# Five tiles from seven products to eight, and row loads moved in the order of issue, in a Fourier layer followed by a squared-ReLU MLP

## The chip, the cores and the metric

The kernel runs on one core of a Trainium2 chip. The metric is the time on the device for one execution, in microseconds (us), lower is better. Engines: TensorE (PE in the profile; PEld is its weight load), VectorE (DVE), ScalarE (ACT), GpSimd (POOL) and SyncE (SP), which here only issues DMAs.

## The reference

```python
def _attn_ref(x, w_r, w_i, b_r, b_i):          # x: 8 x 3008 x 256
    X = np.fft.rfft(x, axis=1)
    Yr = X.real @ w_r - X.imag @ w_i + b_r
    Yi = X.real @ w_i + X.imag @ w_r + b_i
    lam = 0.01
    Yr = np.sign(Yr) * np.maximum(np.abs(Yr) - lam, 0.0)
    Yi = np.sign(Yi) * np.maximum(np.abs(Yi) - lam, 0.0)
    return np.fft.irfft(Yr + 1j * Yi, n=x.shape[1], axis=1)

def _moe_ref(x, w_in, w_out, s, b):            # x: 24064 x 256, w_in: 256 x 2048, w_out: 2048 x 256
    r = np.maximum(x @ w_in, 0.0)
    return (s * (r * r) + b) @ w_out
```

A Fourier transform along the sequence of each of eight batches, a complex matrix product with a soft threshold per frequency, the transform back, and then for all 24064 tokens a two-layer network whose activation is a squared ReLU.

## The kernel before

**The Fourier part.** 3008 = 94 x 32, so a transform is done in steps of small matrix products, batch by batch. Step 1 (`s1_units`, 16 units a batch) multiplies x by a 94-point table and stores the rows `u` to a scratch `ud` in DRAM. `take_rows` (L640) loads them back in another order, as four tiles `us` (384 KB each), from a pool of four buffers. Steps 2 and 3 (`s23_units`) do the 32-point transform, reading `us[(b, i // 3)]` for the i-th of 12 forward units, the complex product, the threshold (`shrink`, in a ring of tiles, with small SBUF to SBUF DMAs) and the inverse 32-point transform, and store `v` to `vd` in DRAM. After the last inverse unit two loads bring `vd` back as the two halves `vs` (768 KB each, a pool of two). Step 4 (`s4_units`, 14 groups) does the inverse 94-point transform from them into `yt`: groups 0 to 5 read the first half alone, group 6 reads both.

**The network part.** The tokens are cut into 48 tiles of 384 to 512 tokens (`_tile_order`); batches 0 and 1 have six tiles each, later ones five, and the leftovers of two batches make two tail tiles. `first_mm` does a tile's product with `w_in`, 16 blocks of 128 hidden units, into two banks of PSUM (`psh`); ScalarE takes the ReLU to `rt` (L867), and ScalarE (L877) or VectorE (L880) squares it into `gt`. The product with `w_out` follows one tile later, and in one of two ways:

- `second_mms`, eight products: 64 matmuls of 256 columns, `gt` against `w_out_t`, and two additions of the bias (L941) to the output tile `ost`, two stores each, after slots 7 and 15.
- `seven_mms`, the Strassen-Winograd form: 112 matmuls of 128 columns with sums of blocks on both sides. The weight sums (`T_s`) are made once. The sums of `gt` are made for each tile in `s_op`: three additions on VectorE (L976) and one accumulating DMA issued by POOL (`gt<-gt`, L969, 256 KB) for each half of the tile, two of the additions at slots 10 and 11 of the tile's first product, the rest in slots 2 to 5 of the next. `leave` recombines the seven products on VectorE in eight additions (L1008) and one more (L1026), in slots 4, 6, 11 and 15; the four stores follow in slot 15.

`seven(ti)` says which tiles take the second way, 22 of 48: 4 to 7, 10, 11, 15, 16, 18, 21, 22, 24, 27, 30, 33, 34, 36, 39, 41 to 43 and 45.

**The order.** Everything is one instruction stream an engine, written out by hand in slots: 16 slots a tile, one block of `first_mm` each. In a slot come first what `plan` holds for it, then `first_mm` of this tile, then a share of the second product of the tile before. `mark[b]` is the slot at which batch b's first tile begins: 0, 96, 192, 272, 368, 464, 560, 656. For batch b (2 to 7), with s0, s1, s2 = mark[b-2], mark[b-1], mark[b]: step 1 runs from s0 + 36 to s1 - 14, `take_rows` stands at s1 - 9, steps 2 and 3 run from s1 + 2 to s2 - 28, step 4 in the last 15 slots before s2. The tiles s1/16 - 2 and s1/16 - 1 go by seven wherever they have 480 or 512 tokens.

**Who evacuates.** `evac` and the squares pick ScalarE or VectorE while the stream is written: a planner keeps a running load for each of the two (`load`), raised to `pe["now"]`, TensorE's own running time, and takes the one that would be done first, with a lead of 0.4 us for ScalarE.

All loads and stores named here but x and the accumulates are issued by SP, in stream order; an SP issue waits for its own data and buffers only.

Of the kernel before, what the change touches and what calls it, by code (L numbers as in the profile page):

```python
# [9 lines left out]
F16 = mybir.dt.float16  # L10
# [6 lines left out]
N2 = 32  # L17
# [79 lines left out]
def kernel(  # L97
# [521 lines left out]
    def s1_units(b, more_banks=False):  # L619

        ud = dpool.tile([96, N2, D], F16, name="ud", tag="ud")
        hold = {}

        def unit(i):
            c, j = divmod(2 * i, XCH)
            k = j % UCH
            if k == 0:
                hold["u"] = upool.tile([P, UCH, D], F16, name="u", tag="u")
            ps = any_bank() if more_banks else one_bank()
            matmul(  # L630
                ps[0:96, :], A_t[0:N1, :], x16[(b, c)][0:N1, j * D : (j + 2) * D],
                start=True, stop=True,
            )
            u = hold["u"]
            evac(u[0:96, k : k + 2, :], ps[0:96, :].rearrange("p (j d) -> p j d", j=2), 512)
            if k == UCH - 2:
                n = 2 * i + 2
                nc.sync.dma_start(out=ud[:, n - UCH : n, :], in_=u[0:96])

        def take_rows():  # L640
            uv = ud.rearrange("k n d -> (k n) d").rearrange("(q p) d -> p q d", p=P)
            for q in range(4):
                t = uspool.tile([P, 6, D], F16, name="us", tag="us")
                nc.sync.dma_start(out=t, in_=uv[:, 6 * q : 6 * q + 6, :])
                us[(b, q)] = t

        return [lambda i=i: unit(i) for i in range(N2 // 2)], take_rows

    def s23_units(b):

        vd = dpool.tile([NPAIR, P, D], F16, name="vd", tag="vd")
        if not ring:
            ring.append(bigpool.tile([P, 12, 2, D], F16, name="ring", tag="corr"))
        xf = {}
        zt = {}
        hold = {}

        def fwd_unit(i):

            bank = one_bank()  # L660
            ps = bank.rearrange("p (r c j k) -> p r c j k", r=2, c=DC, j=2)
            t = us[(b, i // 3)]
            for j in range(2):
                q = (2 * i + j) % 6
                for dc in range(DC):
                    matmul(
                        ps[:, :, dc, j, :], t[:, q, dc * P : (dc + 1) * P],
                        F_t[:, 2 * i + j, :], start=True, stop=True,
                    )
            xt = xfpool.tile([P, 3, DC, P], F16, name="xf", tag="xf")  # L670
            evac(xt[:, 1:3].rearrange("p r c k -> p (r c k)"), bank, 512)
            nc.vector.tensor_tensor(out=xt[:, 0], in0=xt[:, 1], in1=xt[:, 2], op=ALU.add)  # L672
            work("dve", 0.34)
            xf[i] = xt

        def sum_unit(h):

            ps = one_bank().rearrange("p (i e) -> p i e", i=2)
            for i in range(2):
                for dc in range(DC):  # L680
                    matmul(
                        ps[:, i, :], xf[2 * h + i][:, 0, dc], W_t[:, dc, 0],
                        start=(dc == 0), stop=(dc == DC - 1),
                    )
            s = mpool.tile([P, 2, D], F32, name="s", tag="m")
            nc.scalar.copy(out=s, in_=ps)
            work("act", 0.49)
            hold[h] = s

        def mix_unit(i):  # L690
            ps = one_bank().rearrange("p (r e) -> p r e", r=2)
            xt = xf.pop(i)
            for r in range(2):
                for dc in range(DC):
                    matmul(
                        ps[:, r, :], xt[:, 2 - r, dc], W_g[:, dc, r],
                        start=(dc == 0), stop=(dc == DC - 1),
                    )
            nc.vector.tensor_tensor(  # L699
                out=ring[0][:, i % 4], in0=ps,  # L700
                in1=hold[i // 2][:, i % 2].unsqueeze(1).to_broadcast([P, 2, D]), op=ALU.add,
            )
            work("dve", 0.67)
            if b == 1:
                shrink(i, 1)
            elif i % 2:
                shrink(i - 1, 2)

        def shrink(i, n):

            m0 = 4 + (i % 2 if n == 1 else 0)
            t, m = ring[0][:, i % 4 : i % 4 + n], ring[0][:, m0 : m0 + n]
            lo, hi = (v.unsqueeze(1).to_broadcast([P, n, 2, D]) for v in (low, high))
            nc.vector.tensor_tensor(out=m, in0=t, in1=lo, op=ALU.max)
            nc.vector.tensor_tensor(out=m, in0=m, in1=hi, op=ALU.min)
            nc.vector.tensor_tensor(out=t, in0=t, in1=m, op=ALU.subtract)
            work("dve", 0.21 + 0.8 * n)
            for k in range(i, i + n):
                z = ring[0][:, 6 + k % 6]
                for j in range(2):  # L720
                    for r in range(2):
                        o = z[64 * r : 64 * r + 64, j]
                        a = t[64 * j : 64 * j + 64, k - i, r]
                        if k < H - 2:
                            nc.sync.dma_start(out=o, in_=a)
                        else:
                            nc.vector.tensor_copy(out=o, in_=a)
                            work("dve", 0.13)
                zt[k] = z

        def inv_unit(i):
            ps = one_bank().rearrange("p (j e) -> p j e", j=2)
            z = zt.pop(i)
            for j in range(2):
                matmul(
                    ps[:, j, :], T_t[:, 2 * i + j, :], z[:, j, :], start=True, stop=True
                )
            if i % 2 == 0:
                hold["v"] = vpool.tile([P, 4, D], F16, name="v", tag="v")
            v = hold["v"]  # L740
            h = 2 * (i % 2)
            evac(v[:, h : h + 2, :], ps, 512)
            if i % 2 == 1:
                nc.sync.dma_start(
                    out=vd[2 * i - 2 : 2 * i + 2].rearrange("q p e -> p q e"), in_=v
                )
            if i == H - 1:
                vv = vd.rearrange("q (k n) e -> (q k) (n e)", n=N2)
                for h in range(2):
                    t = vspool.tile([96, HW, D], F16, name="vs", tag="vs")  # L750
                    nc.sync.dma_start(
                        out=t.rearrange("k n e -> k (n e)"),
                        in_=vv[:, h * HW * D : (h + 1) * HW * D],
                    )
                    vs[(b, h)] = t

        units = []

        def put(f, i, n):
            if 0 <= i < n:  # L760
                units.append(lambda: f(i))

        for h in range(H // 2 + 3):
            for i in range(2):
                put(fwd_unit, 2 * h + i, H)
                put(mix_unit, 2 * h - 2 + i, H)
                put(inv_unit, 2 * h - 6 + i, H)
            put(sum_unit, h, H // 2)
            if h == H // 2:
                units += [lambda: None] * 2  # L770
        return units

    def s4_units(b):

# [288 lines left out]
    def seven(ti):  # L1063
        if ti >= len(tiles) - 2 or not halves(ti):
            return False
        firsts = [mark[b] // MC for b in range(2, B)]
        return (
            ti >= firsts[-1] or 4 <= ti < 8 or any(m - 2 <= ti < m for m in firsts)
            or any(ti == m + 1 for m in firsts[1:])
        )  # L1070

    plan = {}
# [27 lines left out]
    plan.setdefault(52, []).append(lambda: emit_load_x(2, chunks=range(3, 4)))  # L1100
    for i in range(4):
        plan.setdefault(38 + 2 * i, []).append(lambda i=i: make_t(i))
    schedule(24, 42, s23_units(1))
    schedule(mark[1] - 12, 16, s4_units(1))
    for b in range(2, B):
        s0, s1, s2 = mark[b - 2], mark[b - 1], mark[b]
        p = s1 - s0
        units, take_rows = s1_units(b)
        schedule(s0 + 36, p - 50, units)
        plan.setdefault(s1 - 9, []).append(take_rows)  # L1110
        p = s2 - s1
        schedule(s1 + 2, p - 30, s23_units(b))
        schedule(s2 - 15 + (p < 90), 14 - (p < 90), s4_units(b))
        if b + 1 < B:
            for c, at in enumerate((10, 14, 26, 54)):
                plan.setdefault(s1 + at, []).append(
                    lambda b=b, c=c: emit_load_x(b + 1, chunks=range(c, c + 1))
                )
# [46 lines left out]
```

## Time and profile before

| | us |
|---|---|
| median of 3 runs | 844.29 |
| the three runs | 842.41, 844.29, 849.45 |
| the profiled execution | 843.5 |
| its span, first to last instruction | 841.7 |

| issued on | DMA | count | KB each |
|---|---|---|---|
| SP | us<-ud | 28 | 384 |
| SP | vs<-vd | 14 | 768 |
| POOL | gt<-gt | 40 and 4 | 256 and 240 |
| SP | ring<-ring | 280 | 32 |

Instructions stand as engine, operation, out<-in by tile names, shape and count; buffer numbers are left out. `psh`, `psa` and `psf` are pools of PSUM banks. All matmuls are recorded under one helper's line, L175, and evacuations under L187 (ScalarE) and L189 (VectorE), so they are told apart by tiles. An arrow `<-DVE ring L699` behind a line names what ended the idle time before it.

### The profile page before, as it was taken

What the parts mean: (1) busy time and instruction counts of PE and PEld (TensorE: products, weight loads), DVE (VectorE), ACT (ScalarE), POOL (GpSimd) and SP (SyncE); (2) the same over time, 40 slices, a digit from 0 to 9 for tenths busy, and PEclk for the clock granted to TensorE, in tenths of its full rate; (3) what the DMA queues carried; (4) which work ended last, traced back from release to release, by engine and by line L of the source; (5) the groups of instructions that cost most, each with busy time, mean ns of one, the idle gap of its engine ahead of it and who ended that gap; (6) DMA issues with size and microseconds to landing.
All of it is one profiled execution on the core that took longest, in us unless ns stands there. A gap on an engine that the chain in (4) does not pass through costs nothing.

```text
span 841.7 us, 19681 instructions
## 1 busy us (share of the span) xinstructions
PE 823.0 (98%) x7710; PEld 599.3 (71%) x7710; DVE 718.2 (85%) x1120; ACT 722.1 (86%) x959; POOL 87.7 (10%) x116
## 2 busy tenths in 40 slices
PE   8999999999999999999999999999999999999997
PEld 7857767777677767776677666777667767767765
DVE  5988989998898888888888888788889888879885
ACT  5998988998899988988899888889879898788882
POOL 4550001110010001100010000100001000001000
PEclk9999999999999999999999999999999999999999
DMA  8954587356873478436773458614565253513322
GB/s 199 180 152 102 124 195 193 63 104 151 202 177 66 107 173 215 105 90 143 188 184 70 96 137 206 168 53 108 131 175 142 51 109 99 144 45 76 71 64 62
DMA packets 116959, 107.70 MB, mean 128 GB/s; under 512 B 12806, under 2 KB 100874, under 8 KB 115522
## 3 DMA queue, kind: packets, MB, share of 16 engines
q1 hardware_dynamic: 102498, 80.55, 33.7%
q0 software_dynamic: 14368, 25.89, 19.4%
q8 instruction: 60, 0.98, 0.5%
q14 instruction: 33, 0.27, 0.1%
HBM read 53.52 MB, written 46.66 MB: 119 GB/s over the span
## 4 chain that ended last, share of the span: by engine, by line
PE 70%; DVE 11%; ACT 8%; DMA 6%; issue 3%; SPq 1%; POOL 0%; DVEq 0%; ACTq 0%; POOLq 0%
PE psh L175 29%; PE psa L175 25%; PE psf L175 15%; ACT rt L867 3%; DVE gt L880 2%; DVE gt L976 2%; ACT gt L877 2%; DMA vd<-v 1%; DMA ring<-ring 1%; DMA x<-in_x_dram 1%; DVE ring L699 1%; DMA vs<-vd 1%; PE psm L175 1%; DMA gt<-gt 1%; DVE s L976 1%
## 5 line engine op out<-in xcount | busy, mean ns | idle before, releaser
L867 ACT ACTIVATE rt<-psh 128x1024 f32<-128x1024 f32 (+2 forms) x384 | 387.0, 1009 | 66.5 <-PE psh L175 64.3
L175 PEld LDWEIGHTS <-gt 128*128 128x128 f16 (+1 forms) x3728 | 305.1, 101 | 167.7 <-DMA gt<-gt 1.2
L175 PE MATMUL psh<-yt,w_in 128*128 128x512 f16 (+1 forms) x1344 | 396.6, 378 | 0.1
L880 DVE TENSOR_TENSOR gt<-rt 128x1024 f16<-128x1024 f32 (+2 forms) x238 | 285.2, 1203 | 61.1 <-ACT rt L867 59.7
L175 PE MATMUL psa<-w_out_t,gt 128*128 128x256 f16 (+3 forms) x2432 | 305.9, 252 | 1.0 <-DMA gt<-gt 1.0
L877 ACT ACTIVATE gt<-rt 128x1024 f16<-128x1024 f32 (+2 forms) x146 | 151.7, 1039 | 3.5
L175 PEld LDWEIGHTS <-w_in 128*128 128x128 f16 x1536 | 136.2, 98 | 25.3 <-issue 2.6
L175 PE MATMUL psa<-T_s,gt 128*128 128x128 f16 (+1 forms) x992 | 83.4, 219 | 0.0
L969 POOL DMA_DIRECT2D gt<-gt x44 | 39.7, 902 | 379.7 <-DVE s L976 200.3
L699 DVE TENSOR_TENSOR ring<-psf,s 128x512 f16<-128x512 f32 x84 | 57.5, 685 | 3.5 <-PE psf L175 2.7
L187 ACT CAST u<-psf 96x512 f16<-96x512 f32 x91 | 52.6, 580 | 9.1 <-PE psf L175 8.9
L187 ACT CAST v<-psf 128x512 f16<-128x512 f32 x82 | 47.5, 582 | 11.1 <-PE psf L175 11.1
L175 PEld LDWEIGHTS <-xf 128*128 128x128 f16 x504 | 46.5, 98 | 8.7 <-DVE xf L672 1.9
L175 PE MATMUL psh<-tail,w_in 128*128 128x512 f16 (+1 forms) x192 | 52.1, 353 | 0.0
L175 PE MATMUL psf<-W_g,xf 128*128 128x256 f16 x336 | 50.4, 272 | 1.0 <-ACT xf L187 1.0
L234 POOL DMA_DIRECT2D x<-in_x_dram x36 | 19.2, 538 | 265.2 <-PE psf L175 264.1
L187 ACT CAST yt<-psf 128x470 f16<-128x470 f32 (+2 forms) x84 | 43.3, 534 | 4.1 <-PE psf L175 2.9
L1008 DVE SCALAR_TENSOR_TENSOR ost<-psa,s_bc,zz 128x256 f32<-128x256 f32 (+1 forms) x84 | 38.1, 479 | 7.2 <-PE psa L175 6.5
L941 DVE SCALAR_TENSOR_TENSOR ost<-psa,s_bc,bias_bc 128x512 f32<-128x512 f32 (+2 forms) x49 | 35.6, 726 | 6.9 <-PE psa L175 5.0
L175 PE MATMUL psf<-x,A_t 94*96 94x512 f16 x102 | 38.9, 381 | 2.0 <-ACT v L187 0.8
L175 PE MATMUL psf<-C_t,vs 96*128 96x94 f16 (+1 forms) x484 | 37.9, 205 | 0.8 <-DMA vs<-vd 0.8
L187 ACT CAST xf<-psf 128x512 f16<-128x512 f32 x62 | 36.2, 584 | 2.1 <-PE psf L175 1.9
(118 smaller groups left out, 810.7 us busy)
## 6 DMA issues: line engine op xcount, KB each, us to landing
out_dram<-ost SPq DMA_DIRECT2D x152, 128.0 KB
ud<-u SPq DMA_DIRECT2D x56, 192.0 KB
us<-ud SPq DMA_DIRECT2D x28, 384.0 KB
vd<-v SPq DMA_DIRECT2D x42, 256.0 KB
vs<-vd SPq DMA_DIRECT2D x14, 768.0 KB
x<-in_x_dram POOLq DMA_DIRECT2D x28, 376.0 KB, 6.1
gt<-gt POOLq DMA_DIRECT2D x40, 256.0 KB, 4.4
ring<-ring SPq DMA_DIRECT2D x280, 32.0 KB
```

The lines of the kernel that those rows point to most:

```text
L175: return nc.tensor.matmul(out, lhs, rhs, **how)
L187: return None, nc.scalar.copy(out=dst, in_=src)
L234: nc.gpsimd.dma_start(out=t[0:N1, i * w : (i + 1) * w], in_=xv[:, c * XCH * D + i * w : c * XCH * D + (i + 1) * w],)
L699: nc.vector.tensor_tensor(out=ring[0][:, i % 4], in0=ps, in1=hold[i // 2][:, i % 2].unsqueeze(1).to_broadcast([P, 2, D]), op=ALU.add,)
L867: nc.scalar.activation(out=rt[:, :, 0:w], in_=ps[:, :, 0:w], func=AF.Relu)
L877: nc.scalar.activation(out=gt, in_=rr, func=AF.Square)
L880: last_square[0] = nc.vector.tensor_tensor(out=gt, in0=rr, in1=rr, op=ALU.mult)
L941: nc.vector.scalar_tensor_tensor(out=ost[0:size, 0:k], in0=ps[0:size, 0:k], scalar=s_bc[0:size], in1=bias_bc[0:size].unsqueeze(1).to_broad ...
L969: nc.gpsimd.dma_start(out=a12, in_=a11, accum_op=ALU.add)
L976: nc.vector.tensor_tensor(out=out, in0=a, in1=b, op=op)
L1008: nc.vector.scalar_tensor_tensor(out=out, in0=of, scalar=s_bc[0:size], in1=other, op0=ALU.mult, op1=ALU.add)
```

## The change

```diff
-        def take_rows():
+        def take_rows(which=range(4)):
             uv = ud.rearrange("k n d -> (k n) d").rearrange("(q p) d -> p q d", p=P)
-            for q in range(4):
+            for q in which:
                 t = uspool.tile([P, 6, D], F16, name="us", tag="us")
                 nc.sync.dma_start(out=t, in_=uv[:, 6 * q : 6 * q + 6, :])
                 us[(b, q)] = t
...
             if i == H - 1:
-                vv = vd.rearrange("q (k n) e -> (q k) (n e)", n=N2)
-                for h in range(2):
-                    t = vspool.tile([96, HW, D], F16, name="vs", tag="vs")
-                    nc.sync.dma_start(
-                        out=t.rearrange("k n e -> k (n e)"),
-                        in_=vv[:, h * HW * D : (h + 1) * HW * D],
-                    )
-                    vs[(b, h)] = t
+                hold["vv"] = vd.rearrange("q (k n) e -> (q k) (n e)", n=N2)
+                take_half(0)
+                if b == 1:
+                    take_half(1)
+
+        def take_half(h):
+            t = vspool.tile([96, HW, D], F16, name="vs", tag="vs")
+            nc.sync.dma_start(
+                out=t.rearrange("k n e -> k (n e)"),
+                in_=hold["vv"][:, h * HW * D : (h + 1) * HW * D],
+            )
+            vs[(b, h)] = t
...
-        return units
+        return units, lambda: take_half(1)
...
         return (
-            ti >= firsts[-1] or 4 <= ti < 8 or any(m - 2 <= ti < m for m in firsts)
-            or any(ti == m + 1 for m in firsts[1:])
+            ti >= firsts[-1] or 4 <= ti < 7 or any(m - 2 <= ti < m for m in firsts)
         )
...
-        plan.setdefault(s1 - 9, []).append(take_rows)
+        for q, at in enumerate((-9, -6, -1, 4)):
+            plan.setdefault(s1 + at, []).append(lambda t=take_rows, q=q: t([q]))
         p = s2 - s1
-        schedule(s1 + 2, p - 30, s23_units(b))
+        units, take_half = s23_units(b)
+        schedule(s1 + 2, p - 30, units)
+        plan.setdefault(s2 - 23, []).append(take_half)
```

- Tiles 7, 18, 24, 30 and 36 go by eight products; 17 stay by seven. `m + 1` in the removed line is the second tile of batches 3 to 6 (tile 42 of batch 7 stays through `firsts[-1]`).
- For batches 2 to 7 the four row loads stand at slots s1 - 9, s1 - 6, s1 - 1 and s1 + 4.
- For batches 2 to 7 the second half of `vs` is loaded at slot s2 - 23, some five slots after the first; batch 1 keeps both together.

The planner's loads follow from the changed stream, so it may give other evacuations and squares to the two engines anywhere after tile 7.

More of the change, by code (lines that the diff above doesn't have):

```diff
@@ L1102 @@
         plan.setdefault(38 + 2 * i, []).append(lambda i=i: make_t(i))
-    schedule(24, 42, s23_units(1))
+    schedule(24, 42, s23_units(1)[0])
     schedule(mark[1] - 12, 16, s4_units(1))
```

## Prediction

> **What bounds the kernel now.** The page's first part comes first, for the share of each engine.
>
> ```profile
> PE 823.0 (98%) x7710; PEld 599.3 (71%) x7710; DVE 718.2 (85%) x1120; ACT 722.1 (86%) x959; POOL 87.7 (10%) x116
> ```
>
> TensorE is at 98%, so nearly every microsecond of matmul issue is a microsecond of the run. VectorE and ScalarE have room on average, so what they cost is seen only where TensorE pauses. I cut the run at the first matmul of each tile (48 stages; stage k holds the first product of tile k and the second product of tile k-1) and read the busy times by window. A stage named here by k starts at the start of its row.
>
> ```profile
> core 0: us, PE busy (x) PEld busy (x) DVE busy (x) ACT busy (x) POOL busy (x), PEclk, DMA share, GB/s
> ...
> 371.24:390.55 19.31, 18.41 (x191) 13.30 (x189) 16.77 (x28) 18.20 (x25) 2.26 (x3) 1.00 0.57 114
> 390.55:408.25 17.70, 17.70 (x127) 12.19 (x125) 16.28 (x27) 15.10 (x22) 0.54 (x1) 1.00 0.60 156
> ...
> 179.57:198.46 18.89, 18.12 (x191) 13.31 (x188) 16.48 (x31) 17.93 (x25) 2.26 (x3) 1.00 0.65 134
> 660.22:677.62 17.40, 17.40 (x139) 12.63 (x137) 14.70 (x24) 14.70 (x19) 0.00 (x0) 1.00 0.22 57
> 677.62:695.47 17.85, 16.85 (x187) 12.53 (x184) 14.88 (x25) 16.52 (x21) 1.71 (x2) 1.00 0.56 123
> ```
>
> Length, then TensorE busy. Stage 19 (371.24) runs the second product of tile 18 by seven: 0.90 idle. Stage 20 (390.55), with a second product by eight and the same kind of work beside it: none. Stages 8 and 37 follow tiles 7 and 36, which the change also takes: 0.77 and 1.00 idle. The clock is 1.00 throughout, so nothing is to be had there. The timeline of TensorE, where stage 19 pauses and where stage 20 runs by eight:
>
> ```profile
> 378.72 0.50 PE L175 MATMUL psa<-T_s,gt 128*128 128x128 f16 x6
> 379.67 0.38 PE L175 MATMUL psf<-ring,T_t 128*128 128x256 f16 x2 [0.46 <-DVE ring L699]
> ...
> 403.46 0.60 PE L175 MATMUL psa<-w_out_t,gt 128*128 128x256 f16 x4
> ```
>
> A record is longer than its issue interval, as matmuls overlap. Six of 128 columns last 0.50, the last of them 0.219 (mean of the form), so the interval is (0.50 - 0.219)/5 = 0.056. Four of 256 columns: (0.60 - 0.272)/3 = 0.109. After six at 0.056 the next could start at 379.06; it started at 379.67, so 0.61 of issue was lost, though only 0.46 shows as idle. Summed this way from the starts, the lost issue is 1.54 in stage 8, 1.55 in each of 19, 25 and 31 and 1.16 in 37: 7.35 us. Why that one pause came is in the chain of waits in order of time:
>
> ```profile
> 374.56 0.60 DVE gt L976
> 375.16 0.61 DVE s L976
> 375.80 0.70 DVE gt L976
> 376.60 0.62 DVE gt L976
> ...
> 379.02 0.61 DVE ring L699
> ...
> 533.38 7.93 DMA gt<-gt
> ```
>
> The four L976 are the sums by seven products of tile 18. They stand in VectorE's order ahead of the ring addition that the matmul waits for. The last line is another matter: an accumulating DMA of tile 27, for which TensorE waited 1.2 us at 541.36.
>
> **The change part by part.** All against the profiled 843.5 us.
>
> Five tiles back to eight (7, 18, 24, 30, 36). Matmul issue: 112 x 0.056 = 6.27 leave, 64 x 0.109 = 6.98 come, +0.71 a tile, **+3.55** on the path, since TensorE has no room. VectorE, a tile: six sums at 0.687 (4.12), seven additions at 0.479 (3.35), one at 0.748 and one at 0.416 leave; two additions at 0.748 (1.50) come: -7.1 us, about 5.8 of it in the stage after the tile and 1.4 at its own end. POOL loses two accumulating DMAs a tile, 0.85 to 0.9 of issue each, and 256 KB each of traffic. That is off the path, but what queued behind them on POOL is the loads of x, which come free no later.
>
> The pauses. What follows the seven products in these five stages is 7.35 lost. With 5.8 us less on VectorE, stage 19 has 16.77 + 18.20 - 5.8 = 29.2 us for two engines in 18.5, 79% of them. Stage 20 carries 31.4 in 17.70, 89%, and lost 0.09 of issue. Stage 14 (34.2 in 19.59, 87%) lost 0.43. Some of stage 19's pauses name ScalarE (94% busy there), not VectorE; the planner gives a square to the engine with the smaller load, so a freed VectorE takes squares at 1.22 for ScalarE's 1.06, and two or three moved bring ScalarE to 15 or 16. So between 0.09 and 0.43 a stage stays, 0.45 to 2.15; nearer to stage 20, I take 1.0: **-6.35**. Next late there is TensorE itself.
>
> A batch's row loads one by one. SP gets nothing new, four issues of some 0.5 us at other places in its order. SP is not tied to the slots: it issued all four as soon as what stood ahead was done.
>
> ```profile
> 531.38 3.60 SPq L644 DMA_DIRECT2D us<-ud  x4
> ```
>
> The plan puts them at slots 7, 10 and 15 of the tile before the batch boundary and 4 of the next. In all six batches that stage's second product is by seven, and its four stores come in slot 15, after the plan's entry. So nothing stands on SP between the first three, and only the fourth moves, behind those stores. The accumulate issued at 533.38 landed after 7.93; where no rows load it takes 3.2 to 3.9. With 384 KB less in the way at the 240 GB/s that this stretch moves, 1.6 us. TensorE waited 1.2: **-1.2**, between 0 and -1.2. The rows themselves are not late: the fourth tile is first read 22 to 32 slots (23 us or more) after its new place, the second 15 slots after. What the fourth load meets instead is the next stage's accumulates, which landed in 3.3 to 6.5 there with 7 us or more until they are read: +1.6 at most, hidden; without that cover up to 1.6 in each of five stages, 8 us.
> The Trainium skill ("DMA: Bandwidth & Descriptors", Queues, rings and completion order) says that each DMA engine takes the queue rows in turn, a packet at a time; then rows on SP's queue would hardly hold an accumulate on POOL's, this term would be 0 and the sum 1.2 higher. The 7.93 against 3.2 to 3.9 speaks against that reading.
>
> Second half of the last step's rows later. Its issue moves past SP's two stores of slot 7 and what ud stores lie there. The first half is awaited in one stage only (16: 0.95 us of issue, after 8.33 us from issue to landing beside the second half). If the second half holds the first up, 0.95 comes back; if the queue serves them in order, nothing. Between 0 and -0.95, I take **-0.4**. The second half is first read 14 slots (14.7 us) after its place; 8.33 to land leaves 6.4, against the longest wait for such a store at the head of SP, 5.7. Hidden, with 0.7 over; at double the landing time it would cost 7.6 in a batch.
>
> Sum: +3.55 - 6.35 - 1.2 - 0.4 = -4.4, so 839.1 on the profiled run's scale. That run lies 0.8 below the median of 844.29, with three times over 7 us; I take 839.4.
>
> **The rivals.**
> (a) The waits move instead of going. ScalarE was busy 18.20 of 19.31 in stage 19, and if the planner fills VectorE with squares at 1.22 each, the bank that a first-step matmul needs is still freed late, at slots 3, 6, 9 and 15 of stages 8, 19, 25, 31 and 37. Then the 6.35 stays, the DMA terms hide behind it, and the price of issue is left: 843.5 + 3.55 = 847.1, slower. It decides where under 0.71 of pause goes in a stage. For it: the pauses that name ScalarE. Against: stage 20. The Trainium skill ("TensorE: Matmul & The Clock Gate", Wait — 56ns, not 53.3ns?) puts warm matmuls at N/2.4 GHz + 2.5 ns, which by itself also prices the change at a loss; the starts here agree (56 and 109 ns) but hold the pauses too.
> (b) Only the tiles count: rows and second half change nothing: 843.5 + 3.55 - 6.35 = 840.7.
> (c) The relief spreads. Stages 12 to 38 lose about 3.6 more in pauses outside the five, mostly under 0.45 each and waiting for VectorE or ScalarE; with those and the 1.0 that I left gone, 839.1 - 4.6 = 834.5.
> (d) The second half is late after all, behind a store: 7.6 in one batch, 846.7 with the rest as forecast.
>
> **How the numbers follow.** Forecast 0.55, (a) 0.17, (b) 0.13, (c) 0.10, (d) 0.05. A measurement of this kernel can tell about 1% from no change: below 835.9 or above 852.7. Only (c) goes below, 0.10 in all. Above comes (a) with new pauses of 1.1 a stage more, or (d) in two batches: 0.07. The rest, 0.83, is within 1%. Range: from just above (c), 835.4, to (a), 847.1; it leaves out most of (c), half of (a) and some of (d).
>
> **What would show it.** Stages 8, 19, 25, 31 and 37 of the new trace hold 64 matmuls of 256 columns in the second product, no L976 and almost no idle TensorE, and are 0.3 to 0.8 shorter; ScalarE in stage 19 falls to 15 or 16; no wait on gt<-gt at stage 28; three row loads still go out together and the fourth later. It is wrong if TensorE still pauses over 0.7 there, if vs<-vd appears among TensorE's waits more than before, or if gt<-gt does in stages 6, 12, 17, 23 or 35.

## The result and the profile after

| | before | after |
|---|---|---|
| median of 8 runs, us | 843.87 | 838.82 |
| lowest and highest, us | 842.41, 849.45 | 837.91, 841.07 |
| the profiled execution, and its span, us | 843.5, 841.7 | 838.19, 836.4 |

The ratio is 0.9932, with a 95% interval of 0.9905 to 0.9959: 0.7% less time, within the 1% that was forecast, 0.6 us below the predicted 839.4. (Ratios here and below are estimated over the runs of both kernels; the two medians alone give 0.9940.)

The page's first part of the changed kernel, then five of its stages by window (columns as before):

```profile
PE 824.2 (99%) x7470; PEld 598.7 (72%) x7470; DVE 698.8 (84%) x1061; ACT 712.2 (85%) x953; POOL 79.8 (10%) x106
```

```profile
core 0: us, PE busy (x) PEld busy (x) DVE busy (x) ACT busy (x) POOL busy (x), PEclk, DMA share, GB/s
179.15:197.43 18.28, 18.27 (x143) 13.19 (x141) 13.74 (x21) 16.58 (x25) 0.56 (x1) 1.00 0.49 114
369.43:388.27 18.84, 18.72 (x142) 13.17 (x140) 13.40 (x20) 16.24 (x24) 0.57 (x1) 1.00 0.42 98
388.27:405.89 17.62, 17.62 (x126) 12.19 (x124) 15.62 (x25) 15.33 (x22) 0.54 (x1) 1.00 0.56 140
...
672.97:690.37 17.40, 17.40 (x137) 12.62 (x135) 13.23 (x20) 14.02 (x19) 0.00 (x0) 1.00 0.39 106
```

They are stages 8, 19, 20 and 37. TensorE is busy longer than before (824.2 against 823.0), for the price of the five tiles, in a span that is 5.3 shorter: idle time went. In stage 19 not only VectorE fell (16.77 to 13.40), ScalarE did too (18.20 to 16.24), although the change takes no work from ScalarE. Stage 20 next to it, whose second product was by eight already, also lost its last 0.08.

Set side by side stage by stage, the two profiled runs differ in these places and nowhere else by more than 0.02 us:

| stages | after minus before, us |
|---|---|
| 8; 19, 25, 31; 37 (the five tiles' second products) | -0.62; -0.46 each; -0.44 |
| 9; 20, 26, 32; 38 (the stages after them) | -0.02; -0.08 each; -0.23 |
| 28 | -1.21 |
| 16 | -0.76 |
| the start and stages 0 to 3 (mostly the loads of x) | -0.4 |

The first two rows make -2.93. Lost issue, summed as in the prediction, fell from 7.35 to 1.29 in the five stages: 0.21 in stage 8, 0.36 in each of 19, 25 and 31, none in 37. 7.35 - 1.29 - 2.44 (the first row) leaves 3.62 for the issue of eight products in five tiles, 0.72 a tile. The largest of what stays in stage 19, in TensorE's timeline:

```profile
373.56 0.39 PE L175 MATMUL psf<-F_t,us 128*128 128x128 f16 x4
374.06 0.38 PE L175 MATMUL psf<-x,A_t 94*96 94x512 f16 x1
```

Four matmuls of 128 columns at 0.056 end their issue 0.22 after 373.56, at 373.78; the matmul of step 1 that comes next started 0.28 after that, with no idle time shown.

What TensorE waits for, in order of the total (total, times, longest):

```profile
PE psm L175 <- DMA x<-in_x_dram: 2.0, 6, 0.5
PE psa L175 <- DVE ost L1012: 1.4, 4, 0.6
PE psa L175 <- DVE ones L241: 1.0, 1, 1.0
PE psa L175 <- DVE z L509: 0.4, 2, 0.2
PE psf L175 <- DMA ring<-ring: 0.3, 1, 0.3
```

Before, the same view had:

```profile
PE psf L175 <- DVE ring L699: 1.8, 5, 0.5
PE psa L175 <- DMA gt<-gt: 1.0, 1, 1.0
PE psf L175 <- ACT xf L187: 1.0, 4, 0.2
PE psf L175 <- DMA vs<-vd: 0.8, 1, 0.8
```

The waits for `gt<-gt` and `vs<-vd` are gone, those for `xf` too, and the ring addition is down to one wait of 0.3.

But at stage 28, whose wait for `gt<-gt` went, the row loads did not move. SyncE's queue and POOL's timeline there (the stage starts at 523.41):

```profile
528.86 3.51 SPq L644 DMA_DIRECT2D us<-ud  x4
```

```profile
526.77 0.91 POOL L973 DMA_DIRECT2D gt<-gt  x1 [3.25 <-PE psh L175]
529.67 0.87 POOL L973 DMA_DIRECT2D gt<-gt  x1 [1.99 <-PE psf L175]
```

All four loads are still issued in one go, 5.45 into the stage (before, 5.06). What moved is the second accumulate: 6.26 into the stage, where before it was at 7.06 (533.38 of a stage that began at 526.32). The two accumulates landed after 4.6 and 6.1; before after 4.5 and 7.9.

### The profile page after: what moved, and what is told of

Same layout as the page of the kernel before. It is cut to its first block, busy times and chain, and to the rows that moved or that the text cites. A ratio compares the mean times of both kernels' runs of the same rounds, so it can differ in the third digit from the quotient of the medians.

```text
span 836.4 us, 19090 instructions
## 1 busy us (share of the span) xinstructions
PE 824.2 (99%) x7470; PEld 598.7 (72%) x7470; DVE 698.8 (84%) x1061; ACT 712.2 (85%) x953; POOL 79.8 (10%) x106
## 4 chain that ended last, share of the span: by engine, by line
PE 81%; DVE 8%; ACT 5%; DMA 3%; issue 2%; POOL 0%; SPq 0%; DVEq 0%; ACTq 0%; POOLq 0%
PE psh L175 33%; PE psa L175 30%; PE psf L175 17%; ACT rt L871 2%; DVE gt L884 2%; DVE gt L980 1%; DMA ring<-ring 1%; DMA x<-in_x_dram 1%; PE psm L175 1%; ACT gt L881 1%; DVE s L980 1%; DVE ost L1012 1%; ACT u L187 1%; DMA vd<-v 0%; DVE zz L1012 0%
## 5 line engine op out<-in xcount | busy, mean ns | idle before, releaser
L884 DVE TENSOR_TENSOR gt<-rt 128x1024 f16<-128x1024 f32 (+2 forms) x254 | 304.9, 1204 | 88.6 <-ACT rt L871 86.8
L175 PE MATMUL psa<-w_out_t,gt 128*128 128x256 f16 (+3 forms) x2512 | 333.1, 258 | 0.0
L881 ACT ACTIVATE gt<-rt 128x1024 f16<-128x1024 f32 (+2 forms) x130 | 134.8, 1037 | 3.2
L187 ACT CAST u<-psf 96x512 f16<-96x512 f32 x96 | 55.7, 581 | 9.3 <-PE psf L175 8.6
L175 PE MATMUL psa<-T_s,gt 128*128 128x128 f16 (+1 forms) x752 | 63.5, 219 | 0.0
L973 POOL DMA_DIRECT2D gt<-gt x34 | 31.1, 916 | 262.3 <-PE psh L175 86.3
L945 DVE SCALAR_TENSOR_TENSOR ost<-psa,s_bc,bias_bc 128x512 f32<-128x512 f32 (+2 forms) x59 | 43.0, 730 | 4.5 <-PE psa L175 2.3
L187 ACT CAST xf<-psf 128x512 f16<-128x512 f32 x67 | 39.1, 584 | 4.3 <-PE psf L175 4.1
L1012 DVE SCALAR_TENSOR_TENSOR ost<-psa,s_bc,zz 128x256 f32<-128x256 f32 (+1 forms) x64 | 28.8, 479 | 5.4 <-PE psa L175 3.6
```

The lines of the kernel that those rows point to most:

```text
L175: return nc.tensor.matmul(out, lhs, rhs, **how)
L187: return None, nc.scalar.copy(out=dst, in_=src)
L881: nc.scalar.activation(out=gt, in_=rr, func=AF.Square)
L884: last_square[0] = nc.vector.tensor_tensor(out=gt, in0=rr, in1=rr, op=ALU.mult)
L945: nc.vector.scalar_tensor_tensor(out=ost[0:size, 0:k], in0=ps[0:size, 0:k], scalar=s_bc[0:size], in1=bias_bc[0:size].unsqueeze(1).to_broad ...
L973: nc.gpsimd.dma_start(out=a12, in_=a11, accum_op=ALU.add)
```

## The experiments

The theory at the outset was the prediction's: the tiles pay -2.8, the rows -1.2, the halves the rest. Against it stood what the trace after had just shown: the rows did not move, and ScalarE fell too.

**The parts alone.** The tiles:

```diff
-            ti >= firsts[-1] or 4 <= ti < 8 or any(m - 2 <= ti < m for m in firsts)
-            or any(ti == m + 1 for m in firsts[1:])
+            ti >= firsts[-1] or 4 <= ti < 7 or any(m - 2 <= ti < m for m in firsts)
```

> The five tiles by eight alone; row loads and the halves stay as before. Theory (the tiles do nearly all of it): stages 8, 19, 25, 31, 37 and the ones after them are 2.9 us shorter together as in the changed kernel; the 0.95 of pause at the vs load in stage 16 stays. The rows did not move in the changed kernel's trace, so the 1.2 us at stage 28 must come from here too: second accumulate of tile 27 issued about 6.3 us into the stage and landed by 12.4, no pause for it. Ratio to before about 0.995. Rival (the prediction's attribution): stage 28 keeps its 1.2 us pause, the accumulate lands 15.0 us into the stage, ratio 0.9965.

Measured: 838.92 against 844.14, ratio 0.9936 (0.9916 to 0.9955), as much as the whole change. The ten stages around the five tiles fell as above, and so did stage 28, by 1.21, with the rows' code as before: its second accumulate was issued 6.25 into the stage. Stage 16 kept a pause of 1.23. So stage 28's gain came with the tiles, not with the rows.

The rows, by the change's two hunks on `take_rows` alone:

> The row loads one by one alone. Theory: the order and the waits on every engine come out as before, so this is the kernel before again; four row loads still go out together in all six batches, ratio 1.000, and stage 28 keeps a pause for the accumulate of about 1.2 us if that pause belongs to the program and not to the one execution. Rival (prediction): the fourth load stands behind the four stores, the accumulate lands 1.6 us sooner, stage 28 is 1.2 us shorter.

Measured: 843.94, ratio 0.9998 (0.9972 to 1.0024). Every engine's instructions, their order and their waits are those of the kernel before; only line numbers differ. SyncE's queue and POOL in stage 28, which starts at 531.12:

```profile
536.42 3.75 SPq L644 DMA_DIRECT2D us<-ud  x4
```

```profile
538.18 0.88 POOL L969 DMA_DIRECT2D gt<-gt  x1 [2.86 <-DVE zz L1026]
```

The four loads go out together and the accumulate at 7.06 into the stage, as before. (The arrow at the accumulate names the addition `zz` only because it ended just before; in the changed kernel the same accumulate went out at 529.67, before that addition had begun.) The order in which the program names these loads is not the order in which SyncE gets them; this part of the change changes nothing. (For this same program the pause at stage 28 was 0.73 and that at stage 16 1.71, against 1.20 and 0.95 before: so much they scatter from run to run. The profiled run, 848.06, also lost 2.9 in stage 9, waiting for small ring DMAs, where before lost nothing.)

The halves, by the hunks on `vs` and `take_half` alone:

> The second half of the last step's rows later, alone. Theory: only two of six batches issue it later (3 to 4 us, in stages 15 and 39), only stage 16 gains: its pause at the vs load falls from 0.95 to about 0.2, 0.8 us in all, ratio 0.999. Rival: the queue serves the halves in order, so stage 16 keeps its 0.95 and what the changed kernel showed there came with the shifted times; ratio 1.000.

Measured: 844.02, ratio 0.9995 (0.9976 to 1.0014); stage 16 still paused 1.29 where about 0.2 was expected, its first half landing 2.89 into the stage. The two loads come apart in two of the six batches only, before stage 16 and before stage 40, by 2.8 to 4.1 us in the kernels with this edit; in the other four the second still follows the first by 0.37. All of the changed kernel but the rows' hunks:

> Tiles and second half without the edit of the rows: the same instructions and waits on every engine as the changed kernel, so a second look at it. Theory: five stages as in the changed kernel to 0.02 us, stage 28 without a pause for the accumulate; first half of vs in stage 16 lands 1.4 to 1.9 us into the stage (later halves so far: 1.42, 1.78, 1.84, but 2.89 in one; together: 2.54 to 3.31 in six), pause at it 0.2. Rival: the landing in stage 16 scatters as much as with the halves together; pause 0.9 or more.

Its program is the changed kernel's, so this is one more run of it: 839.97; stage 16's first half landed 2.12 in and the pause was 0.53, between the two expectations, where the profile after has 0.18. Over the profiles in which nothing else moved the halves of stage 16, the first half landed 2.5 to 3.3 into the stage with the halves together (seven profiles, pauses of 0.95 to 1.71) and 1.4 to 2.9 apart (five, 0 to 1.29). That is some 0.8 us on average, and not in every run.

**Rows that really come later.** With `held` the loads 2 to 4 are tied behind the stage's four output stores in SyncE's order:

```diff
-        plan.setdefault(s1 - 9, []).append(take_rows)
+        plan.setdefault(s1 - 9, []).append(lambda t=take_rows: t([0]))
+        def held(t=take_rows):
+            with tc.issue_after(last_store[0].ins):
+                t([1, 2, 3])
+        plan.setdefault(s1, []).append(held)
```

> The kernel before, with row loads 2 to 4 of each batch really held on SP behind the four stores of the tile before the batch boundary (what the change's edit of the rows did not do). Theory (row loads stand in the accumulate's way): the second accumulate of tile 27 in stage 28, which landed 14.99, 14.52 and 14.11 us into the stage in three executions with all four loads ahead or beside it, lands by 13.3, and its pause of 1.2, 0.7 and 0.3 us is gone; accumulates of stages 5, 11, 16, 22 and 34 land 1 to 2 us sooner as well; no reader of the rows waits; ratio 0.998 to 1.000, since only stage 28 waited. Rival: the landing is set by its late issue (7.06 us into the stage) and POOL; it stays above 14. Second rival: the second load is now late for its first reader 7 to 9 slots after the boundary, and TensorE waits there, ratio above 1.002.

Measured: 852.25 against 843.67, ratio 1.0104 (1.0084 to 1.0124). Stage 28's second accumulate was issued at 7.06 as before, but landed after 3.92 where it had taken 7.93, and the pause was gone: one row load was beside it now, issued 1.7 earlier, and not four. The held loads came beside the next stages' accumulates instead: those of stages 6 and 12 landed after 8.9 to 9.5, where before they took 4.6 to 6.5. So row loads do hold an accumulate up, by a factor of up to two; that much of the prediction's reason holds. (The Trainium skill, "DMA: Bandwidth & Descriptors", Queues, rings and completion order, has each DMA engine serve its queue rows in turn, a packet at a time. The prediction read that as hardly any delay; a doubling beside one other busy queue is what turns would give if the packets were alike, so rule and trace need not disagree; no run here shows the turns themselves.) But now TensorE waits for the rows, as the second rival had it; that wait is first in its list:

```profile
PE psf L175 <- DMA us<-ud: 7.6, 4, 3.4
```

```profile
257.80 0.22 PE L175 MATMUL psa<-T_s,s 128*120 128x128 f16 x1
261.44 0.61 PE L175 MATMUL psf<-F_t,us 128*128 128x128 f16 x4 [3.42 <-DMA us<-ud]
261.84 1.06 PE L175 MATMUL psh<-yt,w_in 128*128 128x512 f16 x2
```

Stages 6, 12, 29 and 35 grew by 2.03, 4.89, 1.70 and 0.92. That is the timeline of stage 12: after 3.42 idle, two matmuls of 512 columns take 1.06 where they take 0.59 elsewhere. The prediction's cover for late rows ("22 to 32 slots" until the fourth tile is read) was not tested by the change, as nothing moved; held back by the stores, rows are late.

**Why the tiles pay.** Three things change together: the price of issue, VectorE's work, and what the planner then chooses. In the changed kernel 26 of its 822 choices between the two engines are other ones, all in stages 8, 18 and 19, 24 and 25, 30 and 31, 36 and 37: 16 squares go from ScalarE to VectorE, and 10 evacuations from VectorE to ScalarE. The next kernel is the whole change with the 822 choices of before written in, `given` being their list:

```diff
-        return max(load["act"], ready) + ta <= max(load["dve"], ready) + td + lean[0]
+        return given.pop(0) == "1"
```

> The whole change, but the planner's 822 choices between ScalarE and VectorE are those of the kernel before, as a fixed list (26 differ from the changed kernel's, all in stages 8, 18 to 19, 24 to 25, 30 to 31, 36 to 37). Theory: both parts are needed; the pauses that named VectorE (0.62 at slot 6 of stages 19, 25, 31; 1.16 in 37) stay away, those that named ScalarE (0.36 at slot 3, 0.15 at slot 9, 0.42 at slot 15) stay: stage 19 about 19.3 us instead of 18.84, the run 1.5 to 2.5 us over the changed kernel, ratio to before about 0.996. Rival one: VectorE's relief alone does it; stage 19 18.8 or less, ratio 0.993. Rival two: only the moved squares do it; all pauses stay, stage 19 above 20.0, ratio above 0.999.

Measured: 842.39, ratio 0.9984 (0.9961 to 1.0007), apart from the 0.9936 (0.9916 to 0.9955) of the tiles alone beside the same runs of before, and 3.6 over the changed kernel where 1.5 to 2.5 was expected. Its stage 19, and the longest idle time that TensorE's timeline shows there:

```profile
369.86:389.22 19.36, 18.98 (x143) 13.18 (x141) 12.60 (x19) 18.09 (x25) 0.57 (x1) 1.00 0.40 87
```

```profile
381.75 0.38 PE L177 MATMUL psf<-F_t,us 128*128 128x128 f16 x4 [0.20 <-ACT s L688]
```

VectorE has 12.60, less than in the changed kernel, and still the stage takes 19.36, no less than before. The pause at slot 6 that the prediction showed is gone; 0.87 of issue stays lost, in slots 3, 9 and 15, and ScalarE, at 18.09, is named for all three. Over the five stages 3.67 of the 7.35 stays lost: 1.08 in stage 8, 0.86 or 0.87 in each of 19, 25 and 31, and nothing in stage 37. Stage 37, whose pause had named VectorE alone, got its whole -0.44 without any moved square. The opposite kernel, before's tiles with the changed kernel's choices:

> The kernel before, all 22 tiles by seven, with the changed kernel's 822 choices between ScalarE and VectorE as a fixed list. Theory (squares can move only because VectorE got room): VectorE becomes the late one in stages 8, 19, 25, 31, 37, 18.5 us busy or more of 19.3; the ScalarE pauses shrink, the one at slot 6 grows past 1.0; stage 19 19.2 or longer, ratio 0.999 to 1.004. Rival (the planner's choices were the whole matter): stage 19 falls to 18.5 or less, as the seven products are 0.71 cheaper, ratio 0.992 or less.

```profile
370.58:389.46 18.88, 18.41 (x190) 13.32 (x188) 17.85 (x29) 16.41 (x24) 2.27 (x3) 1.00 0.57 112
```

Measured: 844.15, ratio 1.0001 (0.9981 to 1.002). Its stage 19 is shorter by 0.43 than before, nearly as much as with the whole change: the squares that ScalarE gave up help even with seven products there, and VectorE, at 17.85, was not yet the limit that the expectation made it. At 18.88 the stage lies between the two expectations. Sums over the ten stages around the five tiles, in the profiles:

| us | choices of before | choices of after |
|---|---|---|
| tiles of before | 181.91 | 180.38 |
| tiles of after | 181.98 | 178.98 |

The tiles by themselves give +0.06 (unrounded), the choices by themselves -1.5, both -2.93. The choices by themselves gain 2.0 in the five stages and lose 0.5 in the ones after. So over the ten stages the relief of VectorE, without squares to fill it, buys just the price of issue, half of the lost issue against 0.72 a tile. (In whole runs the -1.5 is not seen: ratio 1.0001. The profiled run, 841.04, is the fastest of ten that reach up to 848.12.)

Which part of the seven products did the harm? From before, the five tiles' sums of `gt` left out but for one a half, with both accumulates, the planner charged as if they were there:

```diff
+        if ti in (7, 18, 24, 30, 36) and n != 1:
+            if n != 4:
+                work("dve", 0.07 + size / 480.0)
+            return
```

> The kernel before, with four of the six VectorE sums and both accumulates of tiles 7, 18, 24, 30 and 36 left out (their products then read unsummed blocks); the planner is charged as before, so its choices are unchanged. Theory (the sums stand ahead of the ring addition on VectorE): the 0.62 at slot 6 of stages 19, 25, 31 and the 1.16 of stage 37 go; the pauses that name ScalarE (0.36, 0.15, 0.42) stay or shrink little: stage 19 18.6 to 18.8 instead of 19.31, run 2 to 3.5 us faster, ratio 0.996 to 0.9975. Rival: the recombination's additions hold VectorE; stage 19 stays above 19.1, ratio above 0.9985.

Measured: 841.98, ratio 0.9993 (0.9975 to 1.001). Idle times in stage 19 and after it, in TensorE's timeline:

```profile
376.10 0.38 PE L175 MATMUL psf<-x,A_t 94*96 94x512 f16 x1 [0.20 <-ACT v L187]
...
383.42 0.38 PE L175 MATMUL psf<-F_t,us 128*128 128x128 f16 x4 [0.39 <-ACT s L686]
...
390.32 0.60 PE L175 MATMUL psf<-W_g,xf 128*128 128x256 f16 x4 [0.25 <-ACT xf L187]
```

The slot 6 pause fell from 0.62 to 0.10 as expected, and slot 9, whose pause had been 0.15, lost 0.55: the stage gained 0.12 in all, because ScalarE was next. In stage 37 the loss fell from 1.16 to 0.64. The expectation by the sums missed; stage 19, at 19.19, and the ratio are where the rival had them, but its reason, the recombination, is not borne out by the next kernel. With three recombining additions of the five tiles left out instead (groups 1 and 2 of `leave`; the planner charged as before):

> The kernel before, with the three recombining additions of the third to fifth product (1.7 us of VectorE a tile) of tiles 7, 18, 24, 30 and 36 left out; planner charged as before. Theory (sums at slots 2 to 5 make the pause): stage 19 keeps the 0.62 at slot 6 and is 19.1 to 19.3. Rival: pauses at slots 6 to 15 go with these additions, stage 19 18.7 or less.

A single run took 842.77: stage 19 was 19.36, its slot 6 pause 0.63 as before, but stage 37 fell by 1.06. There TensorE waited behind the recombination, and in part behind the sums ahead of it; in 19 the recombination was not what it waited for.

**The price.** From the changed kernel, four further tiles by eight, whose second products lie in stages that hardly paused:

```diff
-        if ti >= len(tiles) - 2 or not halves(ti):
+        if ti >= len(tiles) - 2 or not halves(ti) or ti in (21, 22, 33, 34):
```

> The changed kernel with four more tiles by eight (21, 22, 33, 34), whose following stages lost only 0.19 to 0.24 us each. Theory (a tile by seven pays where what it adds in pauses is under 0.71): each of stages 22, 23, 34, 35 grows by 0.71 less its pause, 0.45 to 0.55; the run is 1.8 to 2.2 us slower than the changed kernel, ratio to before about 0.9957. Rival: any tile back to eight helps, because VectorE is relieved beyond the stage; the run is as fast as the changed kernel or faster, ratio 0.993 or less.

Measured: 841.47, ratio 0.9977 (0.9962 to 0.9992), so 2.65 over the changed kernel's 838.82. Stages 22, 23, 34 and 35 grew by 0.53, 0.49, 0.53 and 0.49, though their pauses, 0.86 together, went: (2.04 + 0.86)/4 = 0.725 a tile. The growth of the four stages is 2.0 of the 2.65, within the expected 1.8 to 2.2. Two waits for DMAs were not among the changed kernel's:

```profile
PE psf L175 <- DMA vs<-vd: 0.9, 1, 0.9
PE psa L175 <- DMA gt<-gt: 0.3, 1, 0.3
```

The second is in stage 44, which grew by 0.54. The first is stage 16 again: the first half came early, at 1.42, and the second at 8.34 was waited for.

**The second half held back.** From the changed kernel, batch 3's second half tied behind the output stores of stage 15, as in the kernel with the held rows:

> The changed kernel with the second half of vs of batch 3 held on SP until behind the stores of stage 15, some 5 to 6 us after the first half instead of 3.5. Theory (halves share the engines, and what one gains the other may lose): the first half lands below 1.5 us into stage 16 and TensorE does not wait for it; the second lands about 8 to 9 us in, and TensorE waits for it at the seventh group, 0.5 to 1.5 us; stage 16 no shorter than the changed kernel's 16.10. Rival: the second half is out of the way and still in time: stage 16 below 16.0.

The first half landed 1.44 into stage 16 and was not waited for; the second was issued at 2.61, 8.3 after the first and not 5 to 6, and landed at 11.93. A single run took 846.41. TensorE's timeline and windows there:

```profile
327.09 0.21 PE L175 MATMUL psf<-C_t,vs 96*128 96x94 f16 x1
331.83 0.49 PE L175 MATMUL psf<-C_t,vs 96*128 96x94 f16 x4 [4.53 <-DMA vs<-vd]
332.12 1.06 PE L175 MATMUL psh<-yt,w_in 128*128 128x512 f16 x2
```

```profile
327.00:332.00 5.00, 0.47 (x9) 0.31 (x7) 1.20 (x3) 1.21 (x2) 0.00 (x0) 0.90 1.03 239
332.00:336.00 4.00, 4.00 (x31) 2.89 (x30) 1.60 (x2) 2.13 (x3) 0.00 (x0) 0.50 1.04 292
336.00:339.00 3.00, 3.00 (x33) 2.21 (x32) 1.76 (x3) 2.06 (x3) 0.00 (x0) 0.70 0.31 82
339.00:343.50 4.50, 4.50 (x59) 3.30 (x57) 3.11 (x5) 4.16 (x6) 0.91 (x1) 1.00 0.00 0
```

The stage grew by 7.5. The direction was expected, the size was not: of the 7.5, some 4.7 is waiting and the rest, some 2.8, the clock, granted at 0.50 for six us behind the wait (the 0.70 of the third row is a mean, of 0.50 up to 337.80 and 1.00 from there).

**More room for VectorE.** The changed kernel with the planner's lead for ScalarE at 0.2 instead of 0.4:

> The changed kernel with the planner's lead for ScalarE at 0.2 us instead of 0.4 (66 of 822 choices change, net 28 fewer on ScalarE). Theory (what pauses are left wait for ScalarE as often as for VectorE): the 0.28 at slot 3 of stages 19, 25, 31 shrinks, others appear; within 1 us of the changed kernel, ratio to before 0.992 to 0.995. Rival: ScalarE is still the late one throughout, 2 us or more faster, ratio 0.991 or less.

Measured: 839.74, ratio 0.9962 (0.9949 to 0.9976). That is within 1 us of the changed kernel, as expected, though the ratio lies above the expected 0.992 to 0.995. Stages 19, 25 and 31 gained another 0.28 each, and 12, 16, 28 and 40 lost 0.67, 0.51, 0.36 and 0.37, waiting for VectorE, with smaller losses in 5, 6, 7, 22 and 34. No version tried beats the changed kernel.

## Why the prediction held, point by point

**The forecast as a whole** held: -4.4 from the profiled run, and -5.3 measured. Of the 0.9 between, 0.4 lies before stage 4, mostly in the first loads of x, which the change doesn't touch, and the rest in the halves (0.36) and the tiles (0.13). Two of its four reasons held less well than the sum.

**The price, +3.55.** Right: 0.72 a tile from the profile after, 0.725 from the four further tiles, for the 0.71 worked out from the records' starts.

**The pauses, -6.35 with 1.0 left.** The size was right: 7.35 fell to 1.29, or -6.06, and the stages that follow gave about 0.5 more that the prediction did not count. With the price that makes -2.93 for a predicted -2.80. The mechanism was half stated. The prediction put the pauses to VectorE's sums ahead of the ring addition and named the squares moved to VectorE (two or three a stage; it was three or four a tile, one of them mostly a stage earlier, and ScalarE in stage 19 fell to 16.24 of the 15 to 16 foreseen) as something that happens besides. The runs showed that most of the gain hangs on them: with the planner's choices held, the tiles' -2.93 becomes +0.06, and with the sums taken out alone the pause goes from slot 6 to slot 9. Only stage 37, with the stage after it, gained without them. There TensorE had waited behind the recombination as well as the sums, which the prediction did not name.

**Rival (a), the waits move.** It is what happens without the planner: then ScalarE at 18.09 of 19.36 keeps 0.87 of lost issue in stage 19. Not all pauses stay, as the rival had it; about half do (3.67 of 7.35), and stage 28's 1.2 goes besides, so that kernel came to 842.39 and not to 847.1.

**The rows, -1.2.** This step failed: "three still go out together and the fourth later" did not happen, in any batch; all four go out as before and the two programs are the same. The number came true by luck, by another path: stage 28 gained 1.21 with the tiles alone. The failing inference was from a slot of the plan to a place in SyncE's order. What lay behind it was sound: with one row load beside it and not four the same accumulate landed after 3.92. The "3.2 to 3.9" that it was set against is too narrow, though: accumulates with no row load near took 3.2 to 4.4 in stages 40 to 46 of before, and up to 7.7 in stages 7 and 8, so row loads are not all that holds them up.

**Stage 28.** The prediction did not have this effect under the tiles. In every profile with the five tiles by eight and the planner's lead as before, and in the one without their accumulates, the second accumulate was issued 6.25 to 6.35 into the stage and landed by 13.8 without a pause over 0.01; in those with the five tiles' accumulates and rows together it was issued at 7.04 to 7.06, landed at 14.1 to 15.0, and TensorE lost 0.32 to 1.20. The accumulate is tile 27's, none of the five, and what it waits for had been done by 5.7 into the stage, the last of it a sum of `gt` on VectorE. From before, that sum and the accumulate:

```profile
531.31 0.69 DVE L976 TENSOR_TENSOR gt<-gt,s 128x1024 f16<-128x1024 f16 x1
533.38 0.88 POOL L969 DMA_DIRECT2D gt<-gt  x1 [2.86 <-DVE zz L1026]
```

The same lateness is in the changed kernel, at another accumulate, in stage 40:

```profile
726.00 0.69 DVE L980 TENSOR_TENSOR gt<-gt,s 128x1024 f16<-128x1024 f16 x1
728.00 0.86 POOL L973 DMA_DIRECT2D gt<-gt  x1 [2.84 <-PE psa L175]
```

In each profile just one accumulate is issued 1.31 to 1.41 after the last thing that it waits for; the others take 0.53 to 0.67, but for one more in some profiles at 0.82 to 0.94. The late one is always the 69th or 70th DMA that POOL issues. With 88 DMAs on POOL that is stage 28's. With the five tiles' ten accumulates gone it falls in stage 40, and with four more tiles by eight in stage 46, and TensorE does not wait for it there. So the 1.21 hangs on where in POOL's order the late issue falls, and not on the work that the five tiles save. What makes that issue late stays open; no kernel was tried that changes POOL's order alone.

**The halves, -0.4, between 0 and -0.95.** Undersized for this run: the wait fell from 0.95 to 0.18, and the stage by 0.76. By the halves alone nothing was gained (1.29), so between 0 and -0.95 was the right range, and the middle a fair place. The edit reaches two batches of six.

**Rival (b), only the tiles count**, at 840.7, is nearest to the cause: the tiles alone gave 838.92. It lacked stage 28 and the stages that follow the five. **Rival (c)**, the relief spreading, was some 0.5 of its 4.6: stages 20, 26, 32 and 38, not all of 12 to 38. **Rival (d)**, the second half late, did not come in the changed kernel, but its cover is thin: the wait came with four more tiles by eight (0.9), and with the second half held (7.5 in one batch, for the 7.6 that the rival gave, yet 2.8 of them from the clock, which it had not priced).

## What to carry to other kernels

Relief of one of two engines that share work may pay no more than its price if the other engine's work can't move there (+0.06 against -2.93 here; the one stage whose pause named no second engine gained without): look for which engine is second before costing a pause at its full length, and test by freezing the choices. A part's place in the source says nothing of the order of the issues until a trace, or the stream itself, shows them moved; compare the streams of the part alone before giving it a term. Where the number is right, run each part alone all the same: here a term of -1.2 came true to the hundredth for a reason that was not the one given.

## What the runs showed of the hardware

A long wait on a transfer cost TensorE more than its length. After 4.53 idle the clock was granted at 0.50 for the next six us, and after 3.42 for 2.7, where a pair of 512-column matmuls took 1.06 for 0.59. The waits for rows of 1.86 and 1.53 in the kernel with the held rows left the four 128-column matmuls behind them at 0.40, their usual length. The clock fell within the wait. This is the wait of 3.42, which began at 258.02:

```profile
260.00:260.70 0.70, 0.00 (x0) 0.00 (x0) 0.00 (x0) 0.00 (x0) 0.00 (x0) 1.00 1.24 164
260.74:264.13 3.39, 2.69 (x17) 2.04 (x18) 0.29 (x1) 1.61 (x2) 0.00 (x0) 0.50 1.28 238
```

So it fell after 2.7 of idle there, and after 3.7 in the wait of 4.53. The Trainium skill ("TensorE: Matmul & The Clock Gate", Part 1: The HAM clock gate (the "warmup" mystery)) puts the limit at about 3.4 us of idle; the four waits agree with it roughly, and the 2.7 lies below it.

A 256 KB accumulating DMA within SBUF landed after 3.92 beside one row load of 384 KB from another engine's queue and after 7.93 beside four. Two loads of 768 KB issued together on one queue seem to hold each other up: their first half landed 2.5 to 3.3 into the stage, against 1.4 to 2.9 when the second came 2.8 to 4.1 later. The two ranges overlap.
